# One evacuation and one selection per batch of PV products, gathered in four 32-partition strips of PSUM, in a two-problem decode attention kernel

## Chip, cores, metric

One core of a Trainium2 chip. The metric is the device time of one execution in microseconds (us). Executions are compared only when they are in the same state; every run quoted here is of the state "fast". The runs were made in several rounds, with the kernel before in each; its medians there are 864.66 to 865.80 us, and a difference between two labels of different rounds carries up to that 1.1 us.

## The reference

Two decode-attention problems, one query per sequence, with results concatenated. Problem A has 32 heads with a K and a V cache each; problem B has 32 query heads on 8 K/V heads (rep = 4). The caches hold 4096 keys of 128 elements in bf16.

```python
q = (x @ wq).reshape(B, 1, 32, 128).transpose(0, 2, 1, 3)          # B = 4, D = 512
scores = einsum("bhqd,bhkd->bhqk", q, k) * 128 ** -0.5             # problem B: k, v repeated 4 times
o = einsum("bhqk,bhkd->bhqd", softmax(scores), v)
out = o.transpose(0, 2, 1, 3).reshape(B, 1, 4096) @ wo
```

K and V make 336 MB of the 352 MB that must be read.

## The kernel before

The kernel runs problem B first, then A. A *unit* is one sequence and one K/V head: 1 MB of K and 1 MB of V. A *batch* is the four units (sequences) of one K/V head; there are 40 batches, 160 units. TensorE (PE) does per unit: 16 transposes of K (line 319, two bf16 seen as one f32), 32 score matmuls (line 366), 8 PV matmuls (line 497). A scheduler written in the kernel fixes the order on each engine; PV of a unit runs seven units after its transposes.

PV takes the probabilities as the stationary operand, 4 x rep columns at a time (4 key blocks), against 512 columns of V. Its product in PSUM (`dbank`) therefore holds, on 4 x rep partitions, four blocks of which only the diagonal ones are wanted. A copy takes it to SBUF and four small matmuls against a 0/1 matrix `sel` pick and sum the diagonal blocks. The copy is called the evacuation below, the four matmuls the selection. The kernel before does this for each of 156 units (the last four go another way, "stat", which the change leaves alone; the code is shortened):

```python
# emit_PVbig(u)
dps = dbank[kd % ND][0:4 * rep, 0:512]
for g in range(NG4):                                   # 8 matmuls
    c0 = (un["i"] * J + 4 * g) * rep
    pe.matmul(dps, ptb[:, c0:c0 + 4 * rep], vbuf[:, 4 * g * 128:(4 * g + 4) * 128],
              start=(g == 0), stop=(g == NG4 - 1))
# ... directly behind it, in the queue of DVE or ACT:
dst = d_sb[di % NDS][0:4 * rep, :]
use_act = True if rep > 1 else (di % 2 == 1)
t_ev = copy(dst, dps)                                  # DVE tensor_copy or ACT activation(Copy), waits for PV

# emit_SEL(u), one unit later on PE
for jj in range(4):
    pe.matmul(ocols, dsrc[0:4 * rep, jj * 128:(jj + 1) * 128], sel_c[rep][0:4 * rep, jj, :],
              start=(jj == 0), stop=(jj == 3))
# ... emit_norm: DVE divides by the row sums; emit_proj, once per batch:
pdst = dbank[kd % ND][0:Bsz, 0:DOUT]
for hh in range(rep):
    pe.matmul(pdst, onT[pi][:, hq, :], wo_sb[pi][:, hq, :], start=(hh == 0), stop=(hh == rep - 1))
```

Loads come from one queue, in the order of need; a load of K or V is issued when PE has freed one of 6 K or 7 V buffers.

## Time and profile before

| | before |
|---|---|
| time, median of the first 4 runs (later 13) | 865.53 us (865.03) |
| PE busy / DVE / ACT | 96% / 48% / 37% |
| loads | 409 GB/s mean, 415 to 421 in most of the steady slices |
| last landing of a load / end of span (profiled run) | 860.2 / 864.1 us |

In the profiles PE is TensorE, PEld its loads of the stationary operand (they overlap PE), DVE VectorE, ACT ScalarE, POOL GpSimd and SP SyncE. The first fence is from the page of the kernel before: busy time of each engine; GB/s in 40 equal slices; the chain of work that ended last, by engine and by line; then groups of instructions with their shapes, count, busy us, mean ns of one, and the engine's idle time just before them.

```profile
...
PE 826.4 (96%) x10224; PEld 582.5 (67%) x10224; DVE 415.1 (48%) x823; ACT 320.2 (37%) x583; POOL 2.9 (0%) x14
...
GB/s 361 392 410 415 420 416 421 416 395 401 402 419 419 421 419 416 421 419 421 420 419 421 418 416 421 418 421 420 420 421 415 421 419 419 420 421 419 421 402 204
...
PE 87%; DMA 10%; DVE 2%; ACT 1%; issue 0%; SPq 0%; DVEq 0%
PE tb L319 34%; PE dbank L497 32%; PE sbank L366 13%; DMA kn<-in_B_k_cache_dram 5%; DMA vn<-in_A_v_cache_dram 5%; PE om L569 3%; PE dbank L623 2%; PE om L425 1%; PE om L584 1%; DVE ebuf L464 1%; PE tb L265 1%; PE om L399 1%; DVE rowsum L469
...
L497 PE MATMUL dbank<-vn,pt 128*4 128x512 bf16 (+1 forms) x1248 | 303.1, 387 | 1.6 <-DMA vn<-in_A_v_cache_dram 1.6
...
L517 ACT ACTIVATE dsb<-dbank 4x512 bf16<-4x512 f32 (+1 forms) x78 | 45.7, 586 | 148.3 <-PE dbank L497 148.3
L515 DVE CAST scr<-dbank 4x512 bf16<-4x512 f32 x62 | 42.1, 679 | 99.3 <-PE dbank L497 99.3
...
L569 PE MATMUL om<-sel,dsb 4*128 4x1 bf16 (+1 forms) x312 | 19.3, 162 | 0.5 <-ACT dsb L517 0.5
...
```

The page seems to name PE twice: busy 96%, and 87% of the chain. But GB/s is flat. The next fence gives busy us (and instruction counts) of each engine in three stretches of the kernel before, then the granted PE clock, the share of DMA and GB/s.

```profile
...
core 0: us, PE busy (x) PEld busy (x) DVE busy (x) ACT busy (x) POOL busy (x), PEclk, DMA share, GB/s
...
100.00:140.00 40.00, 36.59 (x423) 24.39 (x422) 20.81 (x43) 11.72 (x15) 0.00 (x0) 0.96 1.02 418
300.00:400.00 100.00, 99.72 (x1254) 70.14 (x1254) 48.78 (x96) 40.80 (x80) 0.00 (x0) 1.00 1.01 419
...
700.00:800.00 100.00, 100.00 (x1231) 70.38 (x1230) 49.31 (x95) 41.27 (x80) 0.00 (x0) 1.00 1.01 420
...
```

In the first stretch (problem B) PE is busy 36.6 of 40 us and the loads run at 418 GB/s; in the others (problem A) PE has no idle time left and they run at 419 and 420. The rate does not follow PE. The Trainium skill's page "Perfetto Trace Analysis", section "Identifying the Most-Contended Engine", warns that matmul busy share is no measure of how near PE is to its limit.

Waits of the kernel before (who waited for whom: us in total, times, longest us). The evacuations stood at the head of their queues until PV had finished, and PE itself hardly waited for K:

```profile
...
ACT dsb L517 <- PE dbank L497: 148.3, 78, 5.6
...
DVE scr L515 <- PE dbank L497: 99.3, 62, 1.9
...
ACT scr L517 <- PE dbank L497: 43.0, 16, 3.9
...
PEld tb L319 <- DMA kn<-in_B_k_cache_dram: 10.4, 5, 3.2
...
```

One unit of problem A on PE (start, duration in us, line and shapes), the one with the projection, L623:

```profile
...
541.18 2.10 PE L319 MATMUL tb<-ident_f,kn 128*128 128x128 f32 x16
543.11 0.94 PE L366 MATMUL sbank<-qz,kt 128*128 128x2 bf16 x32
543.98 1.89 PE L497 MATMUL dbank<-vn,pt 128*4 128x512 bf16 x8
545.71 0.38 PE L623 MATMUL dbank<-wo,onT 128*4 128x512 bf16 x1
546.02 0.25 PE L569 MATMUL om<-sel,scr 4*128 4x1 bf16 x4
546.20 2.10 PE L319 MATMUL tb<-ident_f,kn 128*128 128x128 f32 x16
...
```

The starts give a unit's parts: transposes 1.93 us, scores 0.87, then PV, projection and selection up to the next transposes 2.22; the unit takes 546.20 - 541.18 = 5.02 us. The other three units of a batch take 5.16, 5.03 and 4.80 us, so PE's beat is 20.0 us a batch.

### The profile page before, as it was taken

How to read it: one execution, taken by the hardware profiler on the slowest of the kernel's cores; microseconds unless marked ns; L12 is line 12 of the kernel's file. 1: busy time of each engine (PE TensorE's matmuls, PEld its weight loads, DVE VectorE, ACT ScalarE, POOL GpSimd, SP SyncE). 2: the span in 40 equal slices, each digit the busy share in tenths (PEclk: the TensorE clock that was granted, in tenths of full speed). 3: DMA queues.
4: the chain of work that ended last, by engine and by line, in shares of the span. 5: the costliest groups of instructions: out<-in, count | busy, mean ns of one | idle time of the engine just before them, and what ended most of it. 6: DMA issues, size and time to landing. Idle time of an engine off the chain costs nothing.

```text
span 864.1 us, 22450 instructions
## 1 busy us (share of the span) xinstructions
PE 826.4 (96%) x10224; PEld 582.5 (67%) x10224; DVE 415.1 (48%) x823; ACT 320.2 (37%) x583; POOL 2.9 (0%) x14
## 2 busy tenths in 40 slices
PE   6769999999999999999999999999999999999997
PEld 6646665656677667766776777677677577677674
DVE  4544554544445445444544544454455355454442
ACT  2223232324434444333443434344434344344341
POOL 1000000000000000000000000000000000000000
PEclk9699999999999999999999999999999999999999
DMA  9999999999999999999999999999999999999995
GB/s 361 392 410 415 420 416 421 416 395 401 402 419 419 421 419 416 421 419 421 420 419 421 418 416 421 418 421 420 420 421 415 421 419 419 420 421 419 421 402 204
DMA packets 58895, 353.79 MB, mean 409 GB/s; under 512 B 5408, under 2 KB 13616, under 8 KB 17968
## 3 DMA queue, kind: packets, MB, share of 16 engines
q1 hardware_dynamic: 58800, 352.36, 99.4%
q8 instruction: 80, 1.31, 0.6%
q14 instruction: 15, 0.12, 0.0%
HBM read 352.33 MB, written 0.01 MB: 408 GB/s over the span
## 4 chain that ended last, share of the span: by engine, by line
PE 87%; DMA 10%; DVE 2%; ACT 1%; issue 0%; SPq 0%; DVEq 0%
PE tb L319 34%; PE dbank L497 32%; PE sbank L366 13%; DMA kn<-in_B_k_cache_dram 5%; DMA vn<-in_A_v_cache_dram 5%; PE om L569 3%; PE dbank L623 2%; PE om L425 1%; PE om L584 1%; DVE ebuf L464 1%; PE tb L265 1%; PE om L399 1%; DVE rowsum L469 1%; ACT pt L467 1%; DVE kt L339 0%
## 5 line engine op out<-in xcount | busy, mean ns | idle before, releaser
L319 PE MATMUL tb<-ident_f,kn 128*128 128x128 f32 x2560 | 341.2, 282 | 21.4 <-DVE kt L339 11.9
L339 DVE COPY kt<-tb 128x1024 bf16<-128x1024 bf16 x416 | 278.7, 688 | 138.7 <-PE tb L319 132.4
L337 ACT ACTIVATE kt<-tb 128x1024 bf16<-128x1024 bf16 x224 | 225.3, 1026 | 236.7 <-PE tb L319 236.7
L319 PEld LDWEIGHTS tb<-ident_f,kn 128*128 128x128 f32 x2560 | 278.9, 142 | 49.2 <-DVE kt L339 14.3
L497 PE MATMUL dbank<-vn,pt 128*4 128x512 bf16 (+1 forms) x1248 | 303.1, 387 | 1.6 <-DMA vn<-in_A_v_cache_dram 1.6
L497 PEld LDWEIGHTS dbank<-vn,pt 128*4 128x4 bf16 (+1 forms) x1248 | 95.6, 86 | 135.9 <-issue 9.1
L366 PEld LDWEIGHTS sbank<-qz,kt 128*128 128x128 bf16 x5120 | 152.0, 97 | 2.0
L366 PE MATMUL sbank<-qz,kt 128*128 128x2 bf16 (+1 forms) x5120 | 151.0, 164 | 0.0
L517 ACT ACTIVATE dsb<-dbank 4x512 bf16<-4x512 f32 (+1 forms) x78 | 45.7, 586 | 148.3 <-PE dbank L497 148.3
L515 DVE CAST scr<-dbank 4x512 bf16<-4x512 f32 x62 | 42.1, 679 | 99.3 <-PE dbank L497 99.3
L446 ACT ACTIVATE pt<-sbank,nbias 128x32 bf16<-128x32 f32 x128 | 34.9, 285 | 96.9 <-DVE nbias L431 96.8
L638 DVE TENSOR_TENSOR acc_sb<-acc_sb,dbank 4x512 f32<-4x512 f32 x36 | 24.3, 675 | 64.4 <-PE dbank L623 64.4
L569 PEld LDWEIGHTS om<-sel,scr 4*128 4x128 bf16 (+1 forms) x312 | 12.6, 92 | 36.0 <-issue 36.0
L569 PEld LDWEIGHTS om<-sel,dsb 4*128 4x128 bf16 (+1 forms) x312 | 12.5, 91 | 34.1 <-issue 33.5
L446 ACT ACTIVATION_READ_ACCUMULATOR pt<-sbank,nbias 128x1 f32 x128 | 25.9, 202 | 0.0
L387 DVE TENSOR_REDUCE mrow<-sbank 128x4 f32<-128x128 f32 (+1 forms) x40 | 14.8, 371 | 21.9 <-PE sbank L366 21.2
L517 ACT ACTIVATE scr<-dbank 16x512 bf16<-16x512 f32 x16 | 9.4, 586 | 43.0 <-PE dbank L497 43.0
L589 DVE RECIPROCAL rL<-om 128x4 f32<-128x4 f32 (+1 forms) x40 | 7.9, 197 | 31.0 <-PE om L584 31.0
L623 PE MATMUL dbank<-wo,onT 128*4 128x512 bf16 x64 | 20.5, 382 | 0.3 <-DVE onT L598 0.3
L569 PE MATMUL om<-sel,dsb 4*128 4x1 bf16 (+1 forms) x312 | 19.3, 162 | 0.5 <-ACT dsb L517 0.5
L569 PE MATMUL om<-sel,scr 4*128 4x1 bf16 (+1 forms) x312 | 19.3, 162 | 0.0
L425 PE MATMUL om<-diag,ones_f 4*128 4x4 f32 (+1 forms) x80 | 14.5, 250 | 1.3 <-DVE diag L410 1.3
(38 smaller groups left out, 146.0 us busy)
## 6 DMA issues: line engine op xcount, KB each, us to landing
kn<-in_A_k_cache_dram SPq DMA_DIRECT2D x128, 1024.0 KB, 23.8
vn<-in_A_v_cache_dram SPq DMA_DIRECT2D x127, 1024.0 KB, 26.0
kn<-in_B_k_cache_dram SPq DMA_DIRECT2D x32, 1024.0 KB, 16.5
vn<-in_B_v_cache_dram SPq DMA_DIRECT2D x32, 1024.0 KB, 18.0
kn<-in_B_wq_dram SPq DMA_DIRECT2D x4, 1024.0 KB, 16.9
wo<-in_B_wo_dram SPq DMA_DIRECT2D x4, 1024.0 KB, 14.8
kn<-in_A_wq_dram SPq DMA_DIRECT2D x4, 1024.0 KB, 20.2
wo<-in_A_wo_dram SPq DMA_DIRECT2D x4, 1024.0 KB, 15.1
```

Source lines behind the costliest of these rows:

```text
L319: insts.append(pe.transpose(tbf[:, q_ * 128:(q_ + 1) * 128], knf[:, jp * 128:(jp + 1) * 128], ident_f[:, :]))
L337: t_ev = S.add("act", lambda a: [a.activation(dst, src, ACTF.Copy)], [t_pe, war])
L339: t_ev = S.add("dve", lambda v: [v.tensor_copy(dst, src)], [t_pe, war])
L366: insts.append(pe.matmul(sv[:, un["i"], 2 * jp:2 * jp + 2, :], lhsT, qz[p["pi"]][:, un["b"], un["kvh"], par, :, :], start=(par == 0), stop ...
L425: return [pe.matmul(om[t % 2][:, NB_C(t % 2):NB_C(t % 2) + ncols], ones_f[0:ncols, :], diag[t % 2][0:ncols, 0:ncols], start=True, stop=True)]
L446: return [a.activation(pv[:, i, :, hh], sv[:, i, :, hh], ACTF.Exp, bias=nbias[t % 2][:, c:c + 1], scale=scale, accum_out=rowsum[t % 2][:, ...
L497: insts.append(pe.matmul(dps, ptb[:, c0:c0 + 4 * rep], vbuf[:, 4 * g * 128:(4 * g + 4) * 128], start=(g == 0), stop=(g == NG4 - 1)))
L515: t_ev = S.add("dve", lambda v: [v.tensor_copy(dst, dps)], w_ev)
L517: t_ev = S.add("act", lambda a: [a.activation(dst, dps, ACTF.Copy)], w_ev)
L569: return [pe.matmul(ocols, dsrc[0:4 * rep, jj * 128:(jj + 1) * 128], sel_c[rep][0:4 * rep, jj, :], start=(jj == 0), stop=(jj == 3)) for jj ...
L623: insts.append(pe.matmul(pdst, onT[pi][:, hq, :], wo_sb[pi][:, hq, :], start=(hh == 0), stop=(hh == rep - 1)))
L638: bs["acc"] = S.add("dve", lambda v: [v.tensor_tensor(adst, acc_sb[pi][:, :], pdst, op=ALU.add)], wacc)
```

## The change

The intent is to evacuate and select once per batch. The PV of unit i writes partitions 32i and up of one `dbank` (column strip i of the array); one copy of all 128 partitions and four selection matmuls with 16 (problem B) or 4 (A) output columns serve the batch. `sel` gets the matching rows and zeros elsewhere, and `dbank` is zeroed once so that unused rows are finite. The copies also move in their queues: they are now issued one unit after the PV they read, where before they stood right behind it.

```diff
-            dps = dbank[kd % ND][0:4 * rep, 0:512]
+            dps = dbank[t % ND][32 * i:32 * i + 4 * rep, 0:512]
...
-                                           start=(g == 0), stop=(g == NG4 - 1)))
+                                           start=(g == 0), stop=(g == NG4 - 1), tile_position=(0, 32 * i)))
...
-            dst = d_sb[di % NDS][0:4 * rep, :]           # copy per unit, in emit_PVbig
-            use_act = True if rep > 1 else (di % 2 == 1)
...
+        def emit_SELB(bt):                               # once per batch, a unit after its last PV
+            dsrc = d_sb[t % NDS]
+            dps = dbank[t % ND][:, 0:512]
+            if t % 2 == 0:  t_ev = S.add("dve", tensor_copy(dsrc, dps), ...)
+            else:           t_ev = S.add("act", activation(dsrc, dps, Copy), ...)
+            kp = 32 * (n_row - 1) + 4 * rep
+            for jj in range(4):
+                pe.matmul(ocols, dsrc[0:kp, jj * 128:(jj + 1) * 128], sel_c[rep][0:kp, jj, 0:n_row * rep], ...)
...
-            pdst = dbank[kd % ND][0:Bsz, 0:DOUT]         # projection: same strip 0 as before
+            pdst = dbank[t % ND][0:Bsz, 0:DOUT]
```

(The added lines of `emit_SELB` are shortened.) No byte of load is removed.

## The prediction

> **What bounds the kernel now.** The page shows PE busy 96%, and the chain of waits gives PE 87%, so TensorE looks like the limit. I think the loads are. GB/s stays at 415 to 421 from 60 to 840 us, but for one dip (stretches view: DMA share 1.01 to 1.02), whether PE is 91% busy (60 to 140 us) or 100% (300 to 840 us). In the second problem (32 heads) the trace's landings have one unit's K load (1 MB) end 4.97 us after the last one's (K and V, 2.48 us each), with steps of 6.5 us every 16th unit. PE's own beat there is 5.02, 5.16, 5.03, 4.80 us for a batch's four units (timeline), 20.0 us, against 4 x 4.97 = 19.9 plus those steps and a weight load every eighth batch, about 20.4 us. So PE is the slightly faster of two nearly equal streams: K lands 8 us before its transposes at 290 us, but only 0.2 to 2.7 us before them from 540 us on. The last V half lands at 860.2 us and the kernel ends 4 us later. The Trainium skill, "DMA: Bandwidth & Descriptors", section "Bandwidth", gives a fabric ceiling of 435 GB/s and 425 measured for large loads; 420 here agrees with a saturated path.
>
> **What the change does.** Instead of per unit (156 times), dbank is evacuated and selected per batch (39 times), from four 32-partition strips.
> - ACT and DVE: 62 DVE copies of 679 ns (42.1 us) and 94 ACT copies of 586 ns (55.1 us) become about 20 and 19 of the same width (estimate 14 and 11 us). They no longer stand in their queues waiting for PV (99 us of DVE waits, 191 us of ACT waits): the copy is issued a unit later.
> - PE: 624 selection matmuls become 156. In the timeline one selection delays the next work by 0.10 to 0.19 us, so about 0.4 us per batch, 15 to 20 us of PE work in all. PV keeps its shape and its 228 ns each, and only changes its column strip. Two memsets at the start are hidden.
> - 936 of 22450 instructions go; the instruction queue (1.31 MB, 0.6% of DMA) shrinks by about 5%, worth at most 0.7 us.
>
> **Critical path.** None of this shortens the load stream; all bytes stay. PE will run ahead until K is used the moment it lands, then idle. What can reach the end is the last 0.7 us of K slack, and perhaps one instruction fetch.
>
> **Prediction: 864.7 us, 8 in 10 within 861.5 to 867.0 us. Faster by over 2%: 0.03; within 2%: 0.95; slower by over 2%: 0.02.**
>
> **What would show it right or wrong.** Right: GB/s still 419 to 421 in the steady slices; PE busy down to 93 to 95%, with new idle before the transposes released by kn loads (now 9.5 us, all in the first problem); selection and dbank copies at a quarter of their counts; PV still near 380 ns mean; the chain of waits moving from PE to DMA; the tail still 4 us. Wrong: GB/s above 422 with a shorter span (PE set the pace), or PV longer in the shifted strips.
>
> **What would make it wrong.** PE really pacing the loads (then up to 15 us, 2%, is to be gained); strip changes costing PE over 0.15 us a unit; PE idling enough to lose its clock (granted 0.5 around 30 to 40 us, with idle gaps of 2 us).

## The result, and the profile after

The changed kernel takes 864.61 us (median of 9 runs, 864.16 to 865.52) against 865.03 (13 runs). The ratio is 0.9997, 95% interval 0.9987 to 1.0006: the same. Ratios here are the mean time of one kernel's fast runs over that of the other's in the same rounds, so not quite the ratio of the medians quoted.

The same parts of the page, after (the line numbers are those of the changed file: 315 transposes, 493 PV, 523 selection, 514 and 516 the copies, 608 projection):

```profile
...
PE 804.7 (93%) x9756; PEld 565.0 (65%) x9756; DVE 390.5 (45%) x783; ACT 274.8 (32%) x508; POOL 3.2 (0%) x14
...
GB/s 360 392 411 416 420 415 420 415 421 397 401 420 420 421 418 417 421 418 421 421 419 420 418 417 420 420 420 421 420 420 415 418 420 420 419 420 421 420 399 190
...
DMA 54%; PE 43%; DVE 2%; ACT 1%; issue 0%; SPq 0%; DVEq 0%
DMA kn<-in_A_k_cache_dram 38%; PE tb L315 18%; PE dbank L493 15%; DMA vn<-in_A_v_cache_dram 11%; PE sbank L362 6%; DMA kn<-in_B_k_cache_dram 5%; DVE ebuf L460 1%; PE om L421 1%; PE tb L261 1%; DVE rowsum L465 1%; ACT pt L463 1%; DVE kt L335
...
L493 PE MATMUL dbank<-vn,pt 128*4 128x512 bf16 (+1 forms) x1248 | 304.0, 389 | 8.5 <-DMA vn<-in_A_v_cache_dram 8.5
...
L523 PEld LDWEIGHTS om<-sel,scr 100*128 100x128 bf16 (+1 forms) x156 | 6.5, 96 | 17.8 <-issue 16.6
...
```

PE's busy time fell by 21.7 us, 826.4 to 804.7, and the chain went from 87% PE to 54% DMA. PV kept its time, 389 against 387 ns. The selection is in four matmuls for each of 39 batches, 156, where the kernel before had 312 from each of two buffers, 624. The stretches, columns as before:

```profile
...
100.00:140.00 40.00, 36.22 (x412) 25.45 (x411) 21.06 (x47) 8.69 (x10) 0.00 (x0) 0.87 1.01 417
300.00:400.00 100.00, 94.00 (x1149) 65.64 (x1149) 42.51 (x85) 35.86 (x72) 0.00 (x0) 1.00 1.01 419
...
700.00:800.00 100.00, 97.70 (x1177) 68.25 (x1175) 45.53 (x89) 36.39 (x72) 0.00 (x0) 1.00 1.01 420
...
```

PE now has up to 6 us of idle time in 100, at the same 419 and 420 GB/s. (In the stretch of problem B the granted clock is 0.87, not 0.96; more on this below.) The waits show what fills that time:

```profile
...
PEld tb L315 <- DMA kn<-in_A_k_cache_dram: 33.7, 63, 1.6
...
PEld dbank L493 <- DMA vn<-in_A_v_cache_dram: 9.8, 10, 2.1
...
```

PE's weight loads of the transposes now wait for K of problem A, 63 times, 33.7 us in all, and PV for V. Before, no such K wait of problem A existed. The work that was taken from PE came back as waiting for loads. The last V half lands at 859.7 us (before 860.2) and the span ends 3.9 us later, as before, read from the landings in the trace.

The unit with the projection in the changed kernel, taken at a moment when K was there in time:

```profile
...
540.52 2.08 PE L315 MATMUL tb<-ident_f,kn 128*128 128x128 f32 x16
542.43 0.94 PE L362 MATMUL sbank<-qz,kt 128*128 128x2 bf16 x32
543.30 1.24 PE L493 MATMUL dbank<-vn,pt 128*4 128x512 bf16 x5
544.17 0.38 PE L608 MATMUL dbank<-wo,onT 128*4 128x512 bf16 x1
544.38 0.81 PE L493 MATMUL dbank<-vn,pt 128*4 128x512 bf16 x3
545.12 2.13 PE L315 MATMUL tb<-ident_f,kn 128*128 128x128 f32 x16
...
```

It takes 545.12 - 540.52 = 4.60 us against 5.02. Two things are gone between PV and the next transposes: the selection, and the projection as well. L608, which the program issues after all eight PV matmuls, starts after five of them and before the last three. Transposes follow PV's start by 1.82 us, as in a unit without projection.

### The profile page after: what moved, and what is told of

It is laid out like the page before. It is cut to its first block, busy times and chain, and to the rows that moved or that the text cites. A ratio compares the mean times of both kernels' runs of the same rounds, so it can differ in the third digit from the quotient of the medians.

```text
span 863.7 us, 21340 instructions
## 1 busy us (share of the span) xinstructions
PE 804.7 (93%) x9756; PEld 565.0 (65%) x9756; DVE 390.5 (45%) x783; ACT 274.8 (32%) x508; POOL 3.2 (0%) x14
## 3 DMA queue, kind: packets, MB, share of 16 engines
q8 instruction: 76, 1.25, 0.6%
## 4 chain that ended last, share of the span: by engine, by line
DMA 54%; PE 43%; DVE 2%; ACT 1%; issue 0%; SPq 0%; DVEq 0%
DMA kn<-in_A_k_cache_dram 38%; PE tb L315 18%; PE dbank L493 15%; DMA vn<-in_A_v_cache_dram 11%; PE sbank L362 6%; DMA kn<-in_B_k_cache_dram 5%; DVE ebuf L460 1%; PE om L421 1%; PE tb L261 1%; DVE rowsum L465 1%; ACT pt L463 1%; DVE kt L335 0%; PE om L570 0%; PE om L523 0%; PE om L395 0%
## 5 line engine op out<-in xcount | busy, mean ns | idle before, releaser
L315 PE MATMUL tb<-ident_f,kn 128*128 128x128 f32 x2560 | 345.5, 285 | 33.7 <-DVE kt L335 12.8
L335 DVE COPY kt<-tb 128x1024 bf16<-128x1024 bf16 x416 | 278.7, 688 | 163.8 <-PE tb L315 160.5
L315 PEld LDWEIGHTS tb<-ident_f,kn 128*128 128x128 f32 x2560 | 283.2, 144 | 94.7 <-DMA kn<-in_A_k_cache_dram 33.7
L623 DVE TENSOR_TENSOR acc_sb<-acc_sb,dbank 4x512 f32<-4x512 f32 x36 | 24.3, 676 | 54.9 <-PE dbank L493 45.9
L584 DVE TENSOR_TENSOR onT<-om,rL 128x4 bf16<-128x4 f32 (+1 forms) x40 | 6.7, 168 | 75.2 <-PE om L523 70.0
L427 DVE COPY nbias<-om 128x4 f32<-128x4 f32 (+1 forms) x40 | 6.6, 164 | 65.6 <-PE om L421 65.6
L421 PEld LDWEIGHTS om<-diag,ones_f 4*128 4x128 f32 (+1 forms) x80 | 11.7, 183 | 18.2 <-issue 16.6
L608 PE MATMUL dbank<-wo,onT 128*4 128x512 bf16 x64 | 20.5, 381 | 0.3 <-DVE onT L584 0.3
L523 PEld LDWEIGHTS om<-sel,scr 100*128 100x128 bf16 (+1 forms) x156 | 6.5, 96 | 17.8 <-issue 16.6
L463 ACT ACTIVATE pt<-ebuf 128x512 bf16<-128x512 f32 x8 | 5.0, 630 | 33.3 <-DVE ebuf L460 33.3
L570 PE MATMUL om<-rowsum,ones_f 128*128 128x4 f32 (+1 forms) x80 | 15.3, 263 | 0.0
L400 DVE TENSOR_REDUCE gmax<-om 4x1 f32<-4x128 f32 (+1 forms) x40 | 11.2, 279 | 9.0 <-PE om L395 9.0
## 6 DMA issues: line engine op xcount, KB each, us to landing
kn<-in_B_k_cache_dram SPq DMA_DIRECT2D x32, 1024.0 KB, 19.4
```

The source lines that it names most:

```text
L315: insts.append(pe.transpose(tbf[:, q_ * 128:(q_ + 1) * 128], knf[:, jp * 128:(jp + 1) * 128], ident_f[:, :]))
L335: t_ev = S.add("dve", lambda v: [v.tensor_copy(dst, src)], [t_pe, war])
L421: return [pe.matmul(om[t % 2][:, NB_C(t % 2):NB_C(t % 2) + ncols], ones_f[0:ncols, :], diag[t % 2][0:ncols, 0:ncols], start=True, stop=True)]
L463: t_exp = S.add("act", lambda a: [a.activation(pt[t % NPT][:, 0:nel], ebuf[:, 0:nel], ACTF.Exp)], [t_sub] + w0)
L570: bs["peL"] = S.add("pe", lambda pe: [pe.matmul(om[t % 2][:, L_C(t % 2):L_C(t % 2) + ncols], ones_f[:, :], rowsum[t % 2][:, 0:ncols], star ...
L608: insts.append(pe.matmul(pdst, onT[pi][:, hq, :], wo_sb[pi][:, hq, :], start=(hh == 0), stop=(hh == rep - 1)))
```

## Experiments

My theory was that the load stream paces both kernels, and that the change saves PE time that is not on the critical path. The rivals were that PE paces them and the change saves nothing, or that the change gives its saving back somewhere on PE. "hv" in a label means that only half of each V is loaded. That takes a quarter of the cache bytes away, and PE becomes the bound. These runs give a wrong result, and show what the change is worth to PE. Beats (us per unit or batch) are read from the starts of each unit's first transpose in the timeline.

### before_hv and after_hv: take load bytes away

The same edit in both kernels:

```diff
-   vbuf[:, 4 * g * 128:(4 * g + 4) * 128]                       # PV
+   vbuf[:, 4 * (g // 2) * 128:(4 * (g // 2) + 4) * 128]
-   sp.dma_start(dst, src)                                        # V load
+   sp.dma_start(dst[:, 0:J // 2, :], src[:, 0:J // 2, :])
    (the last four units, of the other path, likewise)
```

> The kernel before, with only half of every V load (512 KB in place of 1 MB; PV uses the loaded half twice, so the result is wrong on purpose; every instruction of the engines stays). Theory 'the load stream paces': with a quarter of the bytes gone TensorE becomes the bound; the span shrinks only to what TensorE's own beat allows, 20.0 us per batch of the second problem: 840 to 858 us, GB/s near 320. Rival 'TensorE paces': no change, 863 to 867 us.

> The changed kernel with the same half V loads. Theory 'the load stream paces': the TensorE saving that the full loads hid now shows, 19.3 against 20.0 us per batch of the second problem, 32 batches: 18 to 25 us below the run before_hv, ratio of the two 0.970 to 0.980. Rival 'the change saves TensorE nothing, or gives it back': equal to before_hv within 3 us.

before_hv took 858.08 us (0.1 us above the range that I had given; ratio to the kernel before 0.9925, 0.991 to 0.9939), after_hv 828.15 us (0.9579, 0.9539 to 0.962). GB/s and the chain of before_hv, then of after_hv:

```profile
...
GB/s 361 386 409 405 337 284 271 264 279 390 405 326 326 305 326 290 342 339 317 310 321 311 299 315 367 319 312 322 318 308 292 346 348 311 314 317 315 324 103 51
...
PE 92%; DMA 5%; DVE 2%; ACT 1%; issue 0%; SPq 0%; DVEq 0%
...
```

```profile
...
GB/s 361 385 407 413 337 276 305 260 298 354 398 399 319 327 334 304 348 357 336 326 320 329 316 313 386 329 329 324 329 327 303 347 371 328 325 328 334 328 128 52
...
PE 92%; DMA 5%; DVE 2%; ACT 1%; issue 0%; SPq 0%; DVEq 0%
...
```

The loads run far under 420 now and the chain is 92% PE in both, so PE paces, and here the change is worth 858.08 - 828.15 = 29.9 us, 3.5% (by the medians; the four runs of after_hv scatter from 824.26 to 832.94 us, the slower the lower their mean granted clock, 0.982 to 0.966). So the rival "the change saves PE nothing" falls. The beat of problem A is 20.0 us a batch before and 19.3 after. I had expected 18 to 25 us, so the saving was larger than I thought. Note also how little before_hv gains, 7 us: in the kernel before, PE was only just not the bound.

### before_lite: take PE work away instead

```diff
-                for g in range(NG4):
+                for g in (0, NG4 - 1):        # two of the eight PV matmuls, full loads
```

> The kernel before with full loads and two of the eight PV matmuls per unit (wrong on purpose), 1.37 us less TensorE work per unit, nine times what the change takes away. Load-stream theory: nothing to gain, 861 to 865 us, GB/s still 419 to 421 in the steady slices. Rival 'TensorE paces, the change just saves too little to see': over 100 us faster.

The result is wrong here too. It took 864.15 us; the ratio is 0.9983 (0.9968 to 0.9998), 1.4 us by the medians.

```profile
...
PE 721.2 (84%) x9288; PEld 596.2 (69%) x9288; DVE 419.2 (49%) x823; ACT 325.0 (38%) x583; POOL 2.9 (0%) x14
...
GB/s 359 393 409 417 420 416 420 415 420 398 398 421 420 421 419 416 421 419 421 420 418 421 419 415 421 420 420 421 420 421 416 419 419 420 421 420 420 420 414 195
...
DMA 85%; PE 13%; SPq 1%; DVE 0%; issue 0%; ACT 0%; DVEq 0%
...
```

With PE busy 84% instead of 96%, at a mean clock of 0.835 instead of 0.978, and with GB/s unchanged, the kernel is as fast. There are one to three microseconds at most to be had from PE. The rival "PE paces" falls.

### before_pad1, after_pad1, after_pad2: add PE work

One or two redundant matmuls before each unit's PV (overwritten, so the result stays right):

```diff
+                for _ in range(1):            # pad2: range(2)
+                    insts.append(pe.matmul(dps, ptb[:, c0:c0 + 4 * rep], vbuf[:, 0:512], start=True, stop=True))
                 for g in range(NG4):
```

> The kernel before with one redundant 512-column matmul (0.23 us) ahead of each unit's PV; result stays right. Load-stream theory: TensorE's beat goes to 20.9 us per batch, above the loads' average 20.5 us, so time rises, but by less than the 36 us added: 875 to 892 us. Rival 'TensorE paces': the whole 36 us shows, 898 to 903 us.

> The changed kernel with the same redundant matmul per unit. Load-stream theory: beat 20.2 us per batch, still under the loads' 20.5 us, so the added work is hidden: 864 to 871 us, 12 to 25 us below before_pad1. Rival 'TensorE paces': 36 us more than the changed kernel, about 900 us.

> The changed kernel with two redundant matmuls per unit: batch of the second problem 19.3 + 1.8 = 21.1 us, above the loads' average of 20.5 us, so the headroom is used up: 880 to 898 us, near before_pad1 (892.6). Rival 'the changed kernel has much more headroom than the removed instructions': under 870 us.

| | median us | ratio to the kernel before | batch of problem A, free beat |
|---|---|---|---|
| before_pad1 | 892.63 | 1.0323 (1.0283 to 1.0362) | 20.9 us |
| after_pad1 | 865.88 | 1.0011 (0.9992 to 1.003) | 20.2 us |
| after_pad2 | 893.13 | 1.0317 (1.0286 to 1.0348) | 21.0 us |

The landings of K give the loads' own beat in problem A as 20.5 us a batch: the mean of the last 117 steps is 20.50 us in the kernel before, 20.50 in the changed one and 20.46 in before_lite. (Most steps take 4.97 us a unit; there is a longer one every 16 to 19 units and a weight load every eighth batch.) The kernel before with one pad (20.9) and the changed kernel with two (21.0) have a PE beat above it; the kernel before (20.0) and the changed kernel with one pad (20.2) are below it, and those two take the same time. The same added work costs the kernel before 28 us and the changed kernel nothing. So the change bought headroom, about one 512-column matmul per unit. It is used up at the second, where the changed kernel stands where the other stands with one. before_pad1 came out just above my range, and so did the 26.8 us between it and after_pad1.

### after_hv_strip and before_hv_strip: does the projection run inside PV?

In the changed kernel PV of the moment is in strip 1 while the projection is in strip 0. after_hv_strip puts the projection into strip 1 too; before_hv_strip does the opposite in the kernel before, where PV is always in strip 0.

```diff
-            pdst = dbank[...][0:Bsz, 0:DOUT]
+            pdst = dbank[...][32:32 + Bsz, 0:DOUT]         # matmul with tile_position=(0, 32)
-        out_sb1, acc_sb1 on partitions 0 to 3
+        out_sb1, acc_sb1 on partitions 32 to 35
```

> after_hv with the output projection moved from column strip 0 to column strip 1, the strip that the PV of the same moment uses, so that the two cannot overlap. Theory 'part of the saving is projection matmuls running inside PV of another strip': the batch of the second problem grows from 19.29 to about 19.5 us, and the one of the first problem by up to 0.8 us; 5 to 15 us above after_hv. Rival 'all of the saving is the removed selection matmuls': batch stays 19.29 us, time within 3 us of after_hv apart from its own scatter of 824 to 833.

> before_hv with one thing of the change alone: the output projection goes to column strip 1 while PV stays in strip 0; nothing batched. Theory 'a projection in another strip than PV runs inside PV': the unit with the projection shrinks from 5.02 to about 4.80 us in the second problem, the batch from 20.01 to about 19.79 us, and by up to 0.8 us a batch in the first; 7 to 14 us below before_hv, 843 to 852 us. Rival 'the overlap came from batching or from the longer distance between proj and its producer': batch stays 20.01 us, 856 to 860 us.

after_hv_strip took 842.73 us (0.9742, 0.9719 to 0.9765), 14.6 us more than after_hv. Its timeline, the unit with the projection:

```profile
...
553.92 1.89 PE L493 MATMUL dbank<-vn,pt 128*4 128x512 bf16 x8
555.65 0.38 PE L608 MATMUL dbank<-wo,onT 128*4 128x512 bf16 x1
555.96 2.22 PE L315 MATMUL tb<-ident_f,kn 128*128 128x128 f32 x16
...
```

The projection now follows all eight PV matmuls and the transposes start 2.04 us after PV's start, not 1.82. The unit takes 4.82 us instead of 4.60 in problem A and 5.47 instead of 4.61 in B, which has four projection matmuls. before_hv_strip took 850.0 us (0.9811, 0.9783 to 0.984), 8.1 us less than before_hv, with nothing batched: its unit went from 5.02 to 4.80. Both directions agree: a matmul in another column strip than the PV in flight costs PE almost nothing, and the change got this as a side effect.

### before_hv_onesel and before_hv_both: the removed selections, and what is left

```diff
+            if un["i"] < Bsz - 1 and not is_stat(u + 1):
+                return                     # no selection for the first three units of a batch
     # the last one selects for all columns (values of the last unit, wrong on purpose); all copies stay
```

before_hv_both adds the edit of before_hv_strip.

> before_hv with the selection dropped for the first three units of each batch and one selection of all columns for the last (the values are those of the last unit, wrong on purpose); every per-unit evacuation on DVE and ACT stays. Theory 'TensorE gains by removed selections and by the projection running inside PV, not by fewer evacuations': the selections alone give about 0.4 us a batch, 20.01 to about 19.6 us in the second problem; 843 to 852 us. Rival 'the evacuations matter too': less than 0.2 us a batch, 852 us or more.

> before_hv_onesel with the projection also moved to column strip 1, away from PV's strip 0. Theory as above: the two together reach the changed kernel's beat, 19.3 to 19.4 us a batch, though all per-unit evacuations are still there; 826 to 843 us, near after_hv (828). Rival: 0.3 us a batch or more is still missing, which would be the evacuation batching.

Median and ratio: before_hv_onesel 844.31 us (0.9755, 0.9739 to 0.9771), before_hv_both 834.54 us (0.964, 0.9614 to 0.9666). The beats of problem A's four units tell the parts apart:

| us per unit | with projection | second | third | fourth | batch |
|---|---|---|---|---|---|
| before_hv | 5.02 | 5.16 | 5.03 | 4.80 | 20.01 |
| before_hv_onesel | 4.84 | 5.06 | 4.85 | 4.81 | 19.56 |
| before_hv_strip | 4.80 | 5.16 | 5.03 | 4.81 | 19.80 |
| before_hv_both | 4.62 | 5.23 | 4.85 | 4.81 | 19.51 |
| after_hv | 4.60 | 5.10 | 4.85 | 4.74 | 19.29 |

In time, the selections and the projection together gave 858.08 - 834.54 = 23.5 of the 29.9 us. Removing the selections gives 0.45 us a batch, moving the projection alone 0.21, and both together 0.50, less than their sum because the second unit grows. My expectation of 19.3 to 19.4 us was missed by 0.1 us, and 0.22 us separate before_hv_both from the changed kernel.

One would put these 0.22 us down to the copies, which are still per unit in before_hv_both. The traces say otherwise. Of the 0.22 us, 0.13 are in the second unit: its thirteenth transpose starts 0.34 us after the twelfth, in after_hv 0.21 us (medians over problem A), as it waits for a copy of K on DVE. That copy comes late behind the addition of the projection to its sum (`acc_sb`). Here are both on DVE, in before_hv_both (L645, L339), then in after_hv_strip (L623, L335):

```profile
...
528.35 0.68 DVE L645 TENSOR_TENSOR acc_sb<-acc_sb,dbank 4x512 f32<-4x512 f32 x1 [1.56 <-PE dbank L497]
529.07 1.29 DVE L339 COPY kt<-tb 128x1024 bf16<-128x1024 bf16 x2
...
```

```profile
...
536.47 0.68 DVE L623 TENSOR_TENSOR acc_sb<-acc_sb,dbank 4x512 f32<-4x512 f32 x1 [1.74 <-PE dbank L608]
537.18 1.29 DVE L335 COPY kt<-tb 128x1024 bf16<-128x1024 bf16 x2
...
```

From start to start it is 0.71 us in both, though after_hv_strip has no per-unit copies; it is 0.61 us in after_hv, and 0.61 us too in before_hv_onesel, which has all of them. So the delay goes with what before_hv_both and after_hv_strip share, the projection's sum on partitions 32 and up: it is a side effect of the experiment. (after_hv_strip has it too: 0.09 of the 0.31 us that it adds to a batch are in the second unit, 5.19 instead of 5.10 us.) The other 0.09 us is at the one selection that is left: the transposes start 0.18 us after it in before_hv_both (4 partitions read) and 0.12 us in after_hv (100 partitions), and their first step takes 0.14 instead of 0.17 us. Why it is cheaper was not tested. The 0.72 us a batch of problem A are then 0.45 (selections) + 0.21 (projection) + 0.09 (the cheaper selection) - 0.03 (a longer wait for DVE in the second unit of after_hv than in before_hv). No part of them is seen to come from fewer copies.

### after_hv_evac and after_hv_evac2: put the per-unit copies back

An extra copy of each unit's strip to a scratch, behind its PV, on top of after_hv:

```diff
+            t_x = copy(xd, dps)                # waits for this unit's PV; DVE or ACT
     # evac:  e_ = "act" if (rep > 1 or xcnt % 2 == 1) else "dve"      (as in the kernel before)
     # evac2: e_ = "dve" if (i + t) % 2 == 0 else "act"
```

> after_hv with one extra copy per unit of that unit's strip out of PSUM to a scratch, on the engine and at the place in its queue where the kernel before had its per-unit evacuation. Theory 'TensorE gains by its own removed instructions, the evacuation batching adds nothing to its beat': batch of the second problem stays 19.29 us, 824 to 836 us. Rival 'what TensorE gains comes from freeing DVE and ACT of the copies that stood waiting in their queues': batch back towards 20.0 us, 845 to 860 us.

> Second form of after_hv_evac. There the units kept their 4.60, 5.10, 4.85 us, but in every other batch the selection waited 1.4 us for its own copy on DVE, which stood behind the next unit's extra copy: a fault of how the experiment placed its copies. Here the extra copies alternate so that the one ahead of the batch's own copy is on the other engine. Theory 'the extra copies as such cost TensorE nothing': all batches of the second problem 19.29 us, 822 to 834 us, as after_hv. Rival 'the engines' copy load paces TensorE': batches near 20 us, 845 to 853 us, as in the first form.

They took 848.56 (0.9803, 0.9767 to 0.9839) and 848.36 us (0.9801, 0.9781 to 0.9822): my expectations of 824 to 836 and 822 to 834 failed, and both times are in the range of the rival. The first form lost the whole saving of problem A: its 119 units from number 40 to number 159 took 599.5 us, against 600.3 in before_hv and 577.9 in after_hv. But the batches do not slow down evenly, as the rival would have it. In the first form, every other batch is still 19.29 us and the rest have one unit of 6.18 instead of 4.74. Its timeline there:

```profile
...
562.39 0.68 DVE L510 CAST vn<-dbank 4x512 bf16<-4x512 f32 x1 [1.91 <-PE dbank L496]
563.00 0.67 DVE L528 CAST scr<-dbank 128x512 bf16<-128x512 f32 x1
...
563.72 0.25 PE L537 MATMUL om<-sel,scr 100*128 100x4 bf16 x4 [1.37 <-DVE scr L528]
...
```

The batch's own copy, L528, stood behind the extra copy of the next unit, L510, which waited for PV, and the selection L537 waited for L528. In the second form every other batch is again 19.29 us; in the others a unit takes 5.78 instead of 5.10, another 4.88 instead of 4.74. So half of the batches pay nothing for four extra copies, and the other half pay 0.8 to 1.4 us because a copy that waits for PE stands ahead of one that PE needs. These runs show that the copies' place matters: wrongly placed copies can cost all that the change gains. They show no price of the copies where nothing needs the engine behind them.

## Why the prediction was right, point by point

- **The bound.** Predicted: the loads, in spite of PE's 96%. Shown from three sides: less PE work changes the time by 1.4 us (before_lite; the interval of the ratio says 0.2 to 2.8), fewer bytes let it fall until PE paces at 92% of the chain (before_hv, after_hv), and PE work added within the headroom costs nothing (after_pad1).
- **The time.** Predicted 864.7 us, measured 864.61. That it is within 0.1 us is luck: the nine runs scatter over 1.4 us.
- **The signs.** All came: steady GB/s unchanged, PE busy 93%, new waits of the transposes for K, the chain moved to DMA (54%), PV's mean time near 380 ns (389), the tail (from the last landing to the end) 3.9 us. The copies that waited 99 and 191 us in their queues now wait 2 us (DVE) or not at all (ACT).
- **A size that was off: "15 to 20 us of PE work in all".** Where PE paces the change is worth 30 us. The term that I had costed, the selections, was right: about 0.4 us a batch predicted, 0.45 measured. Two terms were missing from the sum: the projection that slips inside PV of another strip (0.21 us a batch) and the selection that is left, cheaper by 0.09 us than one of the old. The total in problem A is 0.72 us a batch; over the 119 units from number 40 to number 159 the profiled runs of before_hv and after_hv show 600.3 us against 577.9, 22.4 us of the 26.6 between those two runs' spans.
- **A thing that I did not foresee: in problem B PE gained little in its cycle.** In one batch the four units took 5.68, 5.18, 6.84 and 4.81 us before (22.5) and 4.62, 5.14, 8.15 and 4.75 after (22.7). The batches alternate with longer ones, of 25.4 to 25.5 us before; after, two of those three take 25.0 us. The six batches from unit 12 on took 143.9 us before and 140.7 after. The third unit has a stall of 1.7 us in both, in which the transposes wait for DVE (in brackets below, idle us and releaser). Here are the end of the transposes and the PV that follows, from the timelines of the kernel before and then after:

```profile
...
112.61 0.66 PE L319 MATMUL tb<-ident_f,kn 128*128 128x128 f32 x4 [1.70 <-DVE kt L339]
...
114.21 1.89 PE L497 MATMUL dbank<-vn,pt 128*16 128x512 bf16 x8
...
```

```profile
...
107.85 0.66 PE L315 MATMUL tb<-ident_f,kn 128*128 128x128 f32 x4 [1.70 <-DVE kt L335]
...
109.69 3.15 PE L493 MATMUL dbank<-vn,pt 128*16 128x512 bf16 x8
...
```

The eight PV matmuls after the same stall took 3.15 us instead of 1.89, because PE was granted half clock there. In the clock record of the changed kernel, half clock was granted at 108.8 to 112.3, 132.7 to 139.6, 156.6 to 160.0, 180.5 to 187.4 and 204.4 to 207.8 us, 24 us between 92 and 208 us. The kernel before has 136.8 to 140.2 and 184.6 to 188.0, 7 us. The mean granted clock of that stretch is 0.90 after and 0.97 before. It is 0.94 in before_hv, 0.91 in before_hv_strip, 0.90 in after_hv, 0.94 in after_hv_strip and 1.00 in after_hv_evac, so it differs between kernels of nearly the same PE work. With full loads the lower clock goes with the change: the mean over the whole span is 0.954 to 0.971 in all ten listed runs of the changed kernel, and 0.974 to 0.983 in the 28 of the kernel before that the experiments' rounds list. In after_hv_evac the third unit took 6.66 us at full clock; with it, an estimate of the changed kernel's four units is 21.2 us. Which part of the change brings half clock, and by what mechanism, stays open. The prediction had named a lost clock as something that could make it wrong, with PE idling 2 us. It came in problem A as well, outside the stretches shown above: in the changed kernel at 511.6 to 518.4 and 675.5 to 678.9 us, just after PE had stood idle 2.05 and 1.90 us (the kernel before: 676.1 to 679.5 us, after 1.60 us; an idle gap of 1.99 us at 344 us in the changed kernel brought none). With full loads it cost nothing that the time shows.
- **Not resolved.** The shorter instruction stream (1.31 to 1.25 MB) was to be worth at most 0.7 us. The interval of the ratio, -1.1 to +0.5 us, cannot show that.

## What to carry to other kernels

A busy share near 100% and a chain of waits full of one engine do not prove that it paces the kernel: compare the beat of the loads with the beat of the engine, and test it by taking work from one and bytes from the other. A change off the critical path can still be worth having as headroom (here one 512-column matmul per unit), but its worth shows only when the other limit moves. Where one waiting copy stands ahead of another in the queue of an engine, its place can cost more than its duration (in after_hv_evac 1.4 us a batch, for a copy of 0.68 us). And an experiment that moves one thing can bring a delay of its own: compare its trace with that of the kernel it is to explain before the remainder is given a name.

## What the Trainium skill lacked or had wrong

- "TensorE: Matmul & The Clock Gate", Part 3, says that matmuls keep program order in start and end, with no reordering. Here the projection L608, issued after eight PV matmuls of another column strip, is recorded as starting at 544.17 us, before the last three PV matmuls (544.38), and the unit is shorter by what the projection had cost (5.02 to 4.80 us in before_hv_strip). Ends of matmuls are modelled, so the evidence is the starts and the unit's length.
- "TensorEngine Tiling (Array Packing)", Key Properties, says that different tiles can run in parallel. The trace agrees. The page lacks a price for one matmul beside running ones: a 512-column matmul cost about 0.2 us in the strip of the running PV and nearly nothing in another one (four of them in problem B: 5.47 against 4.61 us a unit).
- "TensorE: Matmul & The Clock Gate", Part 1, says that the activity gate of the clock has two factors and works in windows of 3.4 us; the record here agrees (only 1.0 and 0.5, in multiples of 3.4 us). Its table in "Why this matters for your kernels" asks for no idle gaps over about 3 us. Here half clock came in a stretch where the largest idle gap of PE was 1.7 us (once per batch of problem B), so gaps under 3 us were not enough to keep the clock.
- "DMA: Bandwidth & Descriptors", section "Bandwidth", lists 341 GB/s for a load of 1 MB and 425 for 16 MB. Loads of 1 MB, about ten of them queued, held 419 to 421 GB/s in most slices here. The page's row was measured on loads issued from GpSimd; for a queue of such loads from SyncE it is too low.
- No page has the longer steps that the landings of K show every 16 to 19 units (6.5 instead of 4.97 us in the kernel before). In the traces (packet times of the packed trace) each of them, those at weight loads aside, ends 2 to 7 us after every eighth 16 KB packet of the instruction queue began, in the kernel before (such packets at 299.2, 380.7 and 463.3 us, landings at 301.8, 385.5 and 466.5) and in before_lite, which has fewer instructions and longer distances between both. In the changed kernel the longer step is split in two, at the eighth packet and the one next to it. No run tested whether the packets cause the steps.
